# Rearranged operand places, output buffers, weight conversion and store names in a one-core fp32 kernel with two MoE layers

## The chip, the cores and the metric

The kernel runs on one core of one Trainium2 chip. The metric is the device time of one execution in microseconds; lower is better. The engines are named as in the profile: PE (TensorE matmuls; PEld its weight loads), DVE (VectorE), ACT (ScalarE), POOL (GpSimd) and SP (SyncE, whose queue issues nearly all DMAs). Each engine works its own list of instructions in order.

## The reference

Linear attention over 8 batches of 8 heads (576 tokens, head size 64), then two feed-forward layers over 4608 tokens (width 512, inner width 2048), everything in float32. The weights arrive as float64.

```
q_s = exp(q - max(q, -1));  q_s /= sum(q_s, -1) + 1e-9
k_s = exp(k - max(k, seq)); k_s /= sum(k_s, seq) + 1e-9
x = q_s @ (k_s^T @ v)                       # (4608, 512)
h = x @ w_in;  g = h * sigmoid(1.702 * h);  x = g @ w_out          # first layer
h = x @ w2_in; g = max(h, 1) if h >= 1, 0 if h <= -1, else (h + 1)**2 / 4
out = g @ w2_out                                                    # second layer
```

## The kernel before

**Precision and products.** Each fp32 operand is split into a high half (fp32r, a copy on ACT) and a low half (operand minus high half, on DVE), and a product is three matmuls: high·high, high·low, low·high. Most of the matrix products are done in seven block products instead of eight (Strassen's scheme in Winograd's form): the activations are cut into quadrants 11, 12, 21, 22, and the products bear the numbers 1 to 7. Products 7, 6 and 5 need one sum of two quadrants before the split, product 2 one sum after it (for product 4, whose quadrant is 21), products 1, 3 and 4 none. So an operand costs DVE two instructions for products 7, 6, 5, 2 and one for 1, 3, 4.

**The passes, in order of time.** First the attention with the direct product by w_in for four of nine blocks of 512 tokens (`gemm1`, L1038 to L1040). In this pass the converted w_in is also combined into the seven weights (`t_pieces`, through the two buffers `t_raw`, tiles `ts0` and `ts1`; `t3_pieces` makes the weight of product 3, through slot 19). Then *pass 1's pairs* (`gemm_b`, L1367): the other five blocks, in three groups of 2 × 384, 2 × 448, 2 × 448 tokens, each with 4 pieces g of 7 products; the results go through gelu into DRAM (`g0_dram`). Then *pass 2* (`gemm2`, L1519), by w_out of the first layer: 5 groups j of tokens (HALVES: 2 × 512 three times, 2 × 384 twice), each with 7 products in the order 1, 7, 6, 5, 2, 3, 4 and 4 pieces i a product. One *step* is one product and one piece, 12 matmuls; a group has 28 steps. Then two more passes for the second layer (`pass_in`, L605, and `out_pass`, L487), which the diff doesn't touch. The combined weights of the later passes are made during the passes before (`Weights`): a raw load of float64 (L234, L240), a conversion (`conv`, L178 to L191), then sums and splits (`hl`, L282 to L304) whose results go to DRAM (`wp_in`, `wp_out`) and come back as 2 MB loads (`load_weight`, L344). The eight conversions of `in2` lie in pass 2 and use slots 8 to 11 (`W2`).

**SBUF.** Most tiles are numbered slots of [128, 2, 512] fp32. In pass 2 an operand's high and low half take two places of a ring, `RING`, in turn; `at_ring` says which. `GROUPS` are the slots of the quadrants, loaded by `load_g`. Sums of products are kept in the slots that `O_AT` names: c22 (finished at product 5), c11 (product 2), u2, u3. In pass 1's pairs the outputs take their slots from the list `EB`.

**The order.** Nothing is scheduled at run time. All work of the first three passes is put on a list with `add(engine, ns, rank, fn, reads, writes, moves, haste)`, and `Plan.order` writes the engines' queues out by a small simulation: each engine takes, of the pieces that could start first, the one with the lowest rank less haste; a piece waits for the last writer of each name it reads and for writer and readers of each name it writes. Transfers are counted one behind another (`moves`), and 1.9 us are added behind a piece of SP. NEXT is the rank of pass 2's first step, LAST that of pass 1's; `later` puts the conversion behind with a haste of −3. `hand` passes slots from one use to the next. Operands are made LA = 3 ranks ahead of their step.

Of the kernel before, what the change touches and what calls it, by code (L numbers as in the profile page):

```python
# [8 lines left out]
FP32 = mybir.dt.float32  # L9
# [89 lines left out]
def kernel(  # L99
# [15 lines left out]
    P = 128  # L115
# [20 lines left out]

    ident = const.tile([P, P], FP32, name="ident")
    half = const.tile([P, 96], FP32, name="half")[:, :1]
    ctx.enter_context(tc.tile_pool(name="even", bufs=1, side="right")).tile([P, 120], FP32, name="even")


    PROD = (1, 7, 6, 2, 5, 4, 3)
# [240 lines left out]
    def bank(i, name="z"):  # L383
        return rooms["p", i].tile([P, 2, TB], FP32, tag=f"p{i}", name=name)

    O_AT = {"s7": 20, "u2": 21, "c11": 22, "c12": 23, "u3": 20, "c22": 23}
    T_AT = (22, 23)
    C_AT = {p: 4 + 2 * i for i, p in enumerate(PROD)}
    C_AT[PROD[-1]] = 20
# [819 lines left out]
        k, c = AT_W[p]  # L1209
        return ("wh", 4 * c + g, k), ("w", 4 * c + g, k)  # L1210

    t_raw = [sm.tile([P, 512], FP32, tag=f"ts{i}", name=f"ts{i}").rearrange("p (a f) -> p a f", a=2) for i in range(2)]

    def t_pieces(u, g):
        ns = 90 + 1.06 * 512
        rows, k = (2 * g, 2 * g + 2), [u]
        free = tuple(("free", x) for x in ("rq", "fq", "h"))

        def do(engine, fn, reads, writes):
            k[0] += 0.04  # L1220
            add(engine, ns, k[0], fn, reads, writes)

        def part(x):
            return t_raw[x] if isinstance(x, int) else f32(t_at(x[0], *rows)[x[1]])

        def name(x):
            return (("ts", x),) if isinstance(x, int) else w_names(x[0], g)[x[1]:x[1] + 1]

        def dve(o, x, y, op):
            do("DVE", lambda: tt(part(o), part(x), part(y), op), name(x) + name(y), name(o))  # L1230

        def high(p, x):
            do("ACT", lambda: copy(t_at(p, *rows)[0], t_raw[x]), (("ts", x),) + free, w_names(p, g)[:1])

        def low(p, x):
            do("DVE", lambda: tt(t_at(p, *rows)[1], t_raw[x], part((p, 0)), ALU.subtract),
                (("ts", x),) + w_names(p, g)[:1] + free, w_names(p, g)[1:])

        def both(x, y, op):
            dve(0, (x, 0), (y, 0), op)  # L1240
            dve(1, (x, 1), (y, 1), op)
            dve(0, 0, 1, ALU.add)

        both(3, 4, ALU.add)
        high(5, 0)
        dve(1, 0, (1, 0), ALU.subtract)
        dve(1, 1, (1, 1), ALU.subtract)
        high(6, 1)
        low(5, 0)
        low(6, 1)  # L1250
        both(1, 3, ALU.subtract)
        high(7, 0)
        low(7, 0)

    t3 = []

    def t3_pieces(u, g):
        ns, rows, own = 90 + 1.06 * 512, (2 * g, 2 * g + 2), (("t3", g % 2),)

        def at(p, i):  # L1260
            return f32(t_at(p, *rows)[i])

        def mine():
            if not t3:
                t3.append(slot(19))
            return t3[0][:, g % 2].rearrange("p (a f) -> p a f", a=2)

        def step_of(k, x, y, op, names):
            add("DVE", ns, u + k, lambda: tt(mine(), x(), y(), op), names, own)

        step_of(0, lambda: at(2, 0), lambda: at(6, 0), ALU.subtract, w_names(2, g)[:1] + w_names(6, g)[:1])
        step_of(0.1, mine, lambda: at(6, 1), ALU.subtract, own + w_names(6, g)[1:])
        step_of(0.2, mine, lambda: at(2, 1), ALU.add, own + w_names(2, g)[1:])
        to = w_names(3, g)
        add("ACT", ns, u + 0.3, lambda: copy(t_at(3, *rows)[0], mine()), own, to[:1])
        add("DVE", ns, u + 0.4, lambda: tt(t_at(3, *rows)[1], mine(), at(3, 0), ALU.subtract), own + to[:1], to[1:])

    for kind in ("rq", "fq", "h"):
        hand(NM + 0.5, (("free", kind),), tuple((kind, n) for n in range(4)), tuple(("fr", n) for n in range(4)))
    hand(AT[NB - 1][1] + 10.88, sl(19), (('t3', 0), ('t3', 1)))  # L1280
    hand(LAST + 40, (('t3', 0), ('t3', 1)), sl(19))
    for g in range(4):
        t_pieces((20, 29, 38, 47)[g], g)
        t3_pieces(LAST - 2.5 + 4.5 * g, g)


    SRC = {1: "11", 7: "12", 6: "11", 2: "21", 5: "12", 4: "21", 3: "22"}
# [34 lines left out]
    PAIRS = ((384, 0), (448, 768), (448, 1664))  # L1322
    QB = {"11": 20, "12": 21, "22": 22, "21": 23}
    CB = {1: (0, 1), 7: (2, 3), 6: (4, 5), 2: (6, 7), 5: (16, 17), 4: (8, 9), 3: (10, 11)}
    E1, E2 = (24, 25, 26, 18), (19, 20, 21, 22)
    EB = E1 * 4 + (24, 25, 26, 18, 19) * 4
    EB = EB[:32] + (E1 + E2) * 2
    WB = (12, 13, 14, 15)
    x_t, x_ops, zb, tmp_b, e_n = {}, {}, {}, {}, [0]

# [42 lines left out]
    def post_b(s, jj, g, p):  # L1373
# [23 lines left out]
        def finish(make, e, src, src_n, a, t, haste=0):  # L1397
# [9 lines left out]
                for off, m, j, c in parts:  # L1407
                    nc.sync.dma_start(out=g0_dram[j][a * 4 + g][:, :, c], in_=got[0][:, :, off:off + m])

            add("SP", 420 * len(parts), s + 1.3, kept, e, tuple(("g0", x[2]) for x in parts), moves=2.5 * n)  # L1410

        def more(name, a, t):
            e = tmp_b[jj, g, name, "n"]
# [62 lines left out]
    OPENS2 = (1, 7, 5, 4)  # L1476
    GROUPS = tuple(range(12, 16)), tuple(range(4, 8)), tuple(range(4))
    W2 = (8, 9, 10, 11)
    RING = (16, 17, 24, 25, 26, 18, 19)
    LA = 3  # L1480
    steps = [(j, p, i) for j in range(NJ) for p in ORDER for i in range(4)]
    g_t, ops2, zs2, tmp2 = {}, {}, {}, {}
# [7 lines left out]
    def load_g(j, qd, i, rank):  # L1490
# [4 lines left out]
        def fn():  # L1495
# [2 lines left out]
                nc.sync.dma_start(out=t[:, :, off:off + m], in_=g0_dram[jb][h * 4 + i][:, :, c:c + m])  # L1498

        add("SP", 560 * len(parts), rank, fn,  # L1500
            step(int(rank) - 1) + tuple(("g0", jb) for _, _, jb, _ in parts), sl(k), moves=2.5 * n)

    def at_ring(s):
        return tuple(RING[(2 * s + x) % len(RING)] for x in range(2))

    def gemm2(s):
        j, p, i = steps[s]
# [17 lines left out]
    def post2(s, j, p):  # L1525
# [42 lines left out]
            more("c22", "u3")  # L1568
            store("c22", 1, 1)
        elif p == 2:  # L1570
            keep("c11")
            store("c11", 0, 0)
        elif p == 3:
            more("u2", "u2")
            store("u2", 0, 1)
# [12 lines left out]
        load_g(0, "22", i, NEXT - (6.9, 6.8, 5.9, 5.8)[i])  # L1588
        load_g(0, "12", i, NEXT - (4.9, 4.8, 3.9, 3.8)[i])
    w_new2 = Weights("in2", W2)  # L1590
    hand(NEXT + 0.5, sl(*W2), w_new2.names)
    w_new2.everything([NEXT + 3 + 12 * i for i in range(8)], later)
    tail = NEXT + 4 * len(ORDER) * (NJ - 1)
    hand(tail + 3, w_new2.names, sl(*W2))

# [103 lines left out]
```

## Time and profile before

| What | Value |
|---|---|
| median of 3 runs | 1545.35 us (1545.29 to 1548.23) |
| the profiled execution | 1543.8 us, of which the span is 1541.8 us |
| PE busy | 1490.0 us, 97% of the span, 7920 matmuls |
| DVE busy | 1125.3 us, 73% |
| ACT busy | 904.2 us, 59% |
| mean granted clock of PE | 0.995 |
| DMA | 341.16 MB, mean 221 GB/s |

The span runs from the first to the last instruction of the profiled execution; its own time lies 2.0 us above it. A busy time is the union of an engine's instructions, as a share of the span. The line numbers are those of the kernel before; L209 is the helper `tt`, through which all sums and low halves go, and L1190 the helper `copy`.

### The profile page before, as it was taken

Reading aid. Unit: us, or ns where it says so; the run is one execution under the profiler, and the core shown is the slowest. Engines: PE = TensorE matmul, PEld = TensorE weight load, DVE = VectorE, ACT = ScalarE, POOL = GpSimd, SP = SyncE. Lnnn points to the kernel's source line nnn. Section 1 sums busy time; section 2 is a strip of 40 time slices with the busy share of each in tenths; the row PEclk is TensorE's granted clock in tenths of the full one; section 3 lists DMA queues with packets and bytes.
Section 4 is the critical chain, followed back from the end, with each engine's and each line's share of the span. In section 5 each row is a group of like instructions: output and inputs, shape, how many; then the busy total and the mean of one; then the engine's idle time right before and its main releaser. Section 6 shows DMA issues by size and latency. Waiting matters only on the chain.

```text
span 1541.8 us, 21375 instructions
## 1 busy us (share of the span) xinstructions
PE 1490.0 (97%) x7920; PEld 1297.4 (84%) x7920; DVE 1125.3 (73%) x1410; ACT 904.2 (59%) x1140; POOL 6.2 (0%) x27
## 2 busy tenths in 40 slices
PE   5999999999998999999999999999999999999998
PEld 3787777889897778787998788888999888888998
DVE  7999962664617798798776576766774878696885
ACT  5878874565634455554534687777786544343443
POOL 0000000000000000000000000000000000000000
PEclk9999999999999999999999999999999999999999
DMA  9977753878778975767559546464768971534341
GB/s 290 283 222 223 232 185 151 274 235 278 248 282 319 326 260 194 255 189 243 170 193 368 198 180 249 184 225 185 252 221 315 415 250 41 196 101 148 103 124 41
DMA packets 273656, 341.16 MB, mean 221 GB/s; under 512 B 97040, under 2 KB 235792, under 8 KB 270864
## 3 DMA queue, kind: packets, MB, share of 16 engines
q1 hardware_dynamic: 272752, 339.70, 65.1%
q8 instruction: 62, 1.02, 0.3%
q14 instruction: 42, 0.34, 0.1%
q10 hardware_dynamic: 800, 0.10, 0.0%
HBM read 196.08 MB, written 143.65 MB: 220 GB/s over the span
## 4 chain that ended last, share of the span: by engine, by line
PE 77%; DMA 12%; DVE 6%; ACT 2%; issue 2%; SPq 1%; DVEq 0%; ACTq 0%
PE z L605 13%; PE z L487 12%; PE z L1519 10%; PE zx L605 9%; PE zx L487 9%; DVE s L209 5%; PE hps L1038 4%; PE z L1367 4%; PE hps L1040 4%; PE hps L1039 4%; DMA g<-s 3%; PE zx L1367 3%; DMA s<-g 3%; PE zx L1519 3%; DMA wp_in<-s 2%
## 5 line engine op out<-in xcount | busy, mean ns | idle before, releaser
L209 DVE TENSOR_TENSOR s<-s,s 128x1024 fp32r<-128x1024 f32 (+7 forms) x692 | 607.6, 918 | 190.4 <-ACT s L282 40.4
L1519 PE MATMUL z<-s,w 128*128 128x512 f32 (+1 forms) x1440 | 305.3, 370 | 16.4 <-DVE s L209 16.0
L1519 PEld LDWEIGHTS z<-s,w 128*128 128x128 f32 x1440 | 262.3, 189 | 57.3 <-DVE s L209 23.0
L1190 ACT ACTIVATE s<-s 128x1024 fp32r<-128x1024 f32 (+2 forms) x168 | 161.3, 969 | 151.5 <-PE z L1519 89.5
L455 ACT ACTIVATE s<-s 128x1024 fp32r<-128x1024 f32 (+1 forms) x140 | 136.3, 976 | 175.4 <-PE zx L487 62.1
L487 PE MATMUL z<-s,w 128*128 128x512 f32 (+1 forms) x1008 | 210.6, 368 | 0.5 <-DVE s L209 0.5
L605 PE MATMUL z<-s,w 128*128 128x512 f32 (+1 forms) x960 | 207.2, 367 | 2.4 <-ACT s L1190 2.4
L487 PEld LDWEIGHTS z<-s,w 128*128 128x128 f32 x1008 | 183.8, 188 | 25.2 <-DVE s L209 0.9
L605 PEld LDWEIGHTS z<-s,w 128*128 128x128 f32 x960 | 175.0, 188 | 25.2 <-ACT s L1190 2.8
L605 PE MATMUL zx<-s,w 128*128 128x512 f32 (+1 forms) x720 | 157.7, 367 | 0.4 <-issue 0.4
L605 PEld LDWEIGHTS zx<-s,w 128*128 128x128 f32 x720 | 131.3, 188 | 17.6 <-issue 0.8
L487 PE MATMUL zx<-s,w 128*128 128x512 f32 (+1 forms) x648 | 135.1, 367 | 0.0
L487 PEld LDWEIGHTS zx<-s,w 128*128 128x128 f32 x648 | 117.9, 188 | 14.9
L1367 PE MATMUL z<-s,w 128*128 128x448 f32 (+1 forms) x576 | 118.6, 359 | 4.8 <-ACT s L1190 3.7
L1367 PEld LDWEIGHTS z<-s,w 128*128 128x128 f32 x576 | 106.8, 190 | 11.8 <-ACT s L1190 4.4
L1038 PE MATMUL hps<-s,w 128*128 128x512 f32 x256 | 104.7, 409 | 0.2 <-ACT s L1044 0.2
L1040 PE MATMUL hps<-s,w 128*128 128x512 f32 x256 | 100.2, 392 | 0.0
L1039 PE MATMUL hps<-s,w 128*128 128x512 f32 x256 | 100.0, 391 | 0.0
L1367 PE MATMUL zx<-s,w 128*128 128x448 f32 (+1 forms) x432 | 89.2, 357 | 3.2 <-ACT zx L1190 2.2
L282 ACT ACTIVATE s<-s 128x256 fp32r<-128x256 f32 x168 | 64.7, 410 | 38.6 <-DMA wp_in<-s 18.3
L209 DVE TENSOR_TENSOR s<-s,z 128x1024 f32<-128x1024 f32 (+2 forms) x58 | 63.6, 1097 | 32.0 <-PE z L1367 7.4
L1367 PEld LDWEIGHTS zx<-s,w 128*128 128x128 f32 x432 | 78.8, 188 | 9.4 <-ACT zx L1190 3.0
(102 smaller groups left out, 1466.4 us busy)
## 6 DMA issues: line engine op xcount, KB each, us to landing
s<-g SPq DMA_DIRECT2D x96, 512.0 KB, 6.3
g<-s SPq DMA_DIRECT2D x80, 512.0 KB, 2.9
wp_out<-s SPq DMA_DIRECT2D x112, 256.0 KB, 2.9
w<-wp_out SPq DMA_DIRECT2D x14, 2048.0 KB, 12.4
g<-s SPq DMA_DIRECT2D x48, 384.0 KB, 3.7
s<-g SPq DMA_DIRECT2D x48, 384.0 KB, 4.3
s<-in_moe_w_out_dram SPq DMA_DIRECT2D x32, 512.0 KB, 4.7
wp_in<-s SPq DMA_DIRECT2D x56, 256.0 KB, 4.0
```

The lines of the kernel that those rows point to most:

```text
L209: return nc.vector.tensor_tensor(out=o, in0=x, in1=y, op=op)
L282: nc.scalar.activation(out=hi, in_=src, func=ACTF.Copy, scale=-1.0 if neg else 1.0)
L455: first_of[s] = nc.scalar.activation(out=hi, in_=src, func=ACTF.Copy)
L487: nc.tensor.matmul(out=z[:, m, :n], lhsT=a, rhs=b[:, c, :], start=(at is not None and i == 0 and c == 0 and x == 0), stop=(i == 3 and c == ...
L605: nc.tensor.matmul(out=z[:, m, :n], lhsT=a, rhs=b[:, c, :], start=(p in OPENS and c == 0 and x == 0), stop=(c == 1 and x == 2), skip_group ...
L1038: nc.tensor.matmul(out=hps, lhsT=wh, rhs=ah, start=(kk == 0), stop=False)
L1039: nc.tensor.matmul(out=hps, lhsT=wh, rhs=al, start=False, stop=False)
L1040: nc.tensor.matmul(out=hps, lhsT=wl, rhs=ah, start=False, stop=(kk == KD - 1))
L1190: nc.scalar.activation(out=o, in_=x, func=ACTF.Copy)
L1367: nc.tensor.matmul(out=zb[jj, g, a][:, m, :n], lhsT=w[:, f], rhs=y[:, c, :], start=(p in OPENS and c == 0 and x == 0), stop=(c == 1 and x ...
L1519: nc.tensor.matmul(out=zs2[j, a][:, m, :n], lhsT=y, rhs=b[:, c, :], start=(first and c == 0 and x == 0), stop=(i == 3 and c == 1 and x == ...
```

## The change

Seven edits. (1) `t_pieces` and `t3_pieces` work on 256 elements instead of 512, in twice as many pieces; `t_raw` shrinks, and `t3_pieces` uses one new buffer `spare` (the former padding tile `even`, wider) in place of both halves of slot 19. (2) So slot 19 is free for pass 1's first group, and `EB` begins with five output buffers instead of four; in the last list two slots are exchanged. (3) The stores of `g0_dram` get a name for each tile, not for each block, and `load_g` waits for the tile that it reads. (4) `RING` gets slot 22 as eighth place. (5) The sum of product 2 is kept as d11 in slot 23, which c22 also uses. (6) Steps 1 and 2 of pass 2 take slots 8 to 11. (7) The eight conversions of `in2` begin at ranks 17 and 23 of each of the first four groups, instead of every 12 ranks from 3.

```diff
@@ -136,7 +136,7 @@
     half = const.tile([P, 96], FP32, name="half")[:, :1]
-    ctx.enter_context(tc.tile_pool(name="even", bufs=1, side="right")).tile([P, 120], FP32, name="even")
+    spare = ctx.enter_context(tc.tile_pool(name="even", bufs=1, side="right")).tile([P, 376], FP32, name="even")[:, :256]
@@ -383,7 +383,7 @@
-    O_AT = {"s7": 20, "u2": 21, "c11": 22, "c12": 23, "u3": 20, "c22": 23}
+    O_AT = {"s7": 20, "u2": 21, "c11": 22, "c12": 23, "u3": 20, "c22": 23, "d11": 23}
     T_AT = (22, 23)
@@ -1209,11 +1209,11 @@
-    t_raw = [sm.tile([P, 512], FP32, tag=f"ts{i}", name=f"ts{i}").rearrange("p (a f) -> p a f", a=2) for i in range(2)]
...
-    def t_pieces(u, g):
-        ns = 90 + 1.06 * 512
-        rows, k = (2 * g, 2 * g + 2), [u]
+    t_raw = [sm.tile([P, 256], FP32, tag=f"ts{i}", name=f"ts{i}").rearrange("p (a f) -> p a f", a=1) for i in range(2)]
...
+    def t_pieces(u, m):
+        g, ns = m // 2, 90 + 1.06 * 256
+        rows, k = (m, m + 1), [u]
         free = tuple(("free", x) for x in ("rq", "fq", "h"))
@@ -1252,36 +1252,29 @@
-    t3 = []
...
-    def t3_pieces(u, g):
-        ns, rows, own = 90 + 1.06 * 512, (2 * g, 2 * g + 2), (("t3", g % 2),)
+    def t3_pieces(u, m):
+        g, ns, rows, own = m // 2, 90 + 1.06 * 256, (m, m + 1), (("t3",),)
+        x = spare.rearrange("p (a f) -> p a f", a=1)
...
-        def mine():
-            if not t3:
-                t3.append(slot(19))
-            return t3[0][:, g % 2].rearrange("p (a f) -> p a f", a=2)
...
-        def step_of(k, x, y, op, names):
-            add("DVE", ns, u + k, lambda: tt(mine(), x(), y(), op), names, own)
+        def step_of(k, a, b, op, names):
+            add("DVE", ns, u + k, lambda: tt(x, a(), b(), op), names, own)
         step_of(0, lambda: at(2, 0), lambda: at(6, 0), ALU.subtract, w_names(2, g)[:1] + w_names(6, g)[:1])
-        step_of(0.1, mine, lambda: at(6, 1), ALU.subtract, own + w_names(6, g)[1:])
-        step_of(0.2, mine, lambda: at(2, 1), ALU.add, own + w_names(2, g)[1:])
+        step_of(0.1, lambda: x, lambda: at(6, 1), ALU.subtract, own + w_names(6, g)[1:])
+        step_of(0.2, lambda: x, lambda: at(2, 1), ALU.add, own + w_names(2, g)[1:])
         to = w_names(3, g)
-        add("ACT", ns, u + 0.3, lambda: copy(t_at(3, *rows)[0], mine()), own, to[:1])
-        add("DVE", ns, u + 0.4, lambda: tt(t_at(3, *rows)[1], mine(), at(3, 0), ALU.subtract), own + to[:1], to[1:])
+        add("ACT", ns, u + 0.3, lambda: copy(t_at(3, *rows)[0], x), own, to[:1])
+        add("DVE", ns, u + 0.4, lambda: tt(t_at(3, *rows)[1], x, at(3, 0), ALU.subtract), own + to[:1], to[1:])
...
         hand(NM + 0.5, (("free", kind),), tuple((kind, n) for n in range(4)), tuple(("fr", n) for n in range(4)))
-    hand(AT[NB - 1][1] + 10.88, sl(19), (('t3', 0), ('t3', 1)))
-    hand(LAST + 40, (('t3', 0), ('t3', 1)), sl(19))
     for g in range(4):
-        t_pieces((20, 29, 38, 47)[g], g)
-        t3_pieces(LAST - 2.5 + 4.5 * g, g)
+        for m in range(2):
+            t_pieces((20, 29, 38, 47)[g] + m, 2 * g + m)
+            t3_pieces(LAST - 2.5 + 4.5 * g + m, 2 * g + m)
@@ -1322,9 +1315,8 @@
     CB = {1: (0, 1), 7: (2, 3), 6: (4, 5), 2: (6, 7), 5: (16, 17), 4: (8, 9), 3: (10, 11)}
-    E1, E2 = (24, 25, 26, 18), (19, 20, 21, 22)
-    EB = E1 * 4 + (24, 25, 26, 18, 19) * 4
-    EB = EB[:32] + (E1 + E2) * 2
+    E1, E2 = (24, 25, 26, 18), (19, 20, 22, 21)
+    EB = ((24, 25, 26, 18, 19) * 7)[:32] + (E1 + E2) * 2
     WB = (12, 13, 14, 15)
@@ -1407,7 +1399,7 @@
-            add("SP", 420 * len(parts), s + 1.3, kept, e, tuple(("g0", x[2]) for x in parts), moves=2.5 * n)
+            add("SP", 420 * len(parts), s + 1.3, kept, e, tuple(("g0", x[2], a * 4 + g) for x in parts), moves=2.5 * n)
@@ -1476,7 +1468,7 @@
     W2 = (8, 9, 10, 11)
-    RING = (16, 17, 24, 25, 26, 18, 19)
+    RING = (16, 17, 24, 25, 26, 18, 19, 22)
     LA = 3
@@ -1498,10 +1490,12 @@
         add("SP", 560 * len(parts), rank, fn,
-            step(int(rank) - 1) + tuple(("g0", jb) for _, _, jb, _ in parts), sl(k), moves=2.5 * n)
+            step(int(rank) - 1) + tuple(("g0", jb, h * 4 + i) for _, _, jb, _ in parts), sl(k), moves=2.5 * n)
     def at_ring(s):
-        return tuple(RING[(2 * s + x) % len(RING)] for x in range(2))
+        if s in (1, 2):
+            return W2[2 * s - 2], W2[2 * s - 1]
+        return tuple(RING[(2 * max(0, s - 2) + x) % len(RING)] for x in range(2))
@@ -1568,8 +1562,8 @@
         elif p == 2:
-            keep("c11")
-            store("c11", 0, 0)
+            keep("d11")
+            store("d11", 0, 0)
         elif p == 3:
@@ -1588,8 +1582,8 @@
     w_new2 = Weights("in2", W2)
-    hand(NEXT + 0.5, sl(*W2), w_new2.names)
-    w_new2.everything([NEXT + 3 + 12 * i for i in range(8)], later)
+    hand(NEXT + 3.5, sl(*W2), w_new2.names)
+    w_new2.everything([NEXT + 28 * (i // 2) + 17 + i % 2 * 6 for i in range(8)], later)
     tail = NEXT + 4 * len(ORDER) * (NJ - 1)
```

## Rows read from the trace of the kernel before

**Rows 1.** The page, busy us by engine, share of the span, instructions.
```profile
PE 1490.0 (97%) x7920; PEld 1297.4 (84%) x7920; DVE 1125.3 (73%) x1410; ACT 904.2 (59%) x1140; POOL 6.2 (0%) x27
```

**Rows 2.** By stretch (us): busy PE, PEld, DVE, ACT, POOL; clock; DMA share, GB/s.
```profile
31.00:263.94 232.94, 232.78 (x1750) 183.82 (x1749) 191.34 (x271) 178.28 (x203) 3.08 (x10) 1.00 0.74 225
263.94:473.09 209.15, 201.20 (x1022) 187.56 (x1021) 107.11 (x182) 118.87 (x177) 0.00 (x0) 0.99 0.78 264
473.09:843.31 370.22, 352.63 (x1682) 305.79 (x1681) 298.51 (x361) 175.52 (x228) 0.00 (x0) 1.00 0.72 246
```

**Rows 3.** Waits of PE: who waited for whom, us in total, times, longest.
```profile
PE z L1519 <- DVE s L209: 16.0, 16, 1.8
```

**Rows 4.** PE in order of time, pass 2: start, us, shape, count [idle before].
```profile
498.80 5.60 PE L1519 MATMUL z<-s,w 128*128 128x512 f32 x24
504.24 5.60 PE L1519 MATMUL zx<-s,w 128*128 128x512 f32 x24
...
515.12 3.11 PE L1519 MATMUL z<-s,w 128*128 128x512 f32 x13
...
543.15 13.89 PE L1519 MATMUL z<-s,w 128*128 128x512 f32 x60 [0.26 <-DVE s L209]
...
567.29 16.39 PE L1519 MATMUL z<-s,w 128*128 128x512 f32 x71 [1.51 <-DVE s L209]
...
634.70 5.55 PE L1519 MATMUL z<-s,w 128*128 128x512 f32 x16 [1.84 <-DVE s L209]
...
798.23 2.24 PE L1519 MATMUL zx<-s,w 128*128 128x384 f32 x12
800.31 2.24 PE L1519 MATMUL z<-s,w 128*128 128x384 f32 x12
```

**Rows 5.** Stretches of 38 us within pass 2, columns as in rows 2.
```profile
511.00:549.00 38.00, 36.07 (x154) 28.20 (x154) 25.97 (x32) 17.22 (x23) 0.00 (x0) 1.00 1.01 387
...
625.00:663.00 38.00, 36.16 (x152) 29.45 (x151) 30.86 (x38) 17.64 (x23) 0.00 (x0) 0.96 0.62 210
```

**Rows 6.** ACT and SP in order of time, end of pass 1.
```profile
448.97 0.92 ACT L1402 ACTIVATE s<-z 128x896 f32<-128x896 f32 x1 [1.47 <-PE z L1367]
...
458.69 0.80 SPq L1498 DMA_DIRECT2D s<-g  x2
459.58 1.19 SPq L1408 DMA_DIRECT2D g<-s  x2
...
468.19 0.64 SPq L344 DMA_DIRECT2D w<-wp_out  x1
...
475.60 5.65 SPq L234 DMA_DIRECT2D s<-in_moe_w_in_dram  x2
```

**Rows 7.** DVE in order of time, start of pass 2.
```profile
476.54 9.42 DVE L209 TENSOR_TENSOR s<-s,s 128x1024 fp32r<-128x1024 f32 x8 [1.44 <-DMA g<-s]
```

**Rows 8.** ACT and DVE in order of time, group 0 of pass 2.
```profile
516.46 0.42 ACT L282 ACTIVATE s<-s 128x256 fp32r<-128x256 f32 x1 [5.74 <-DMA wp_in<-s]
...
516.91 1.90 DVE L209 TENSOR_TENSOR s<-s,s 128x256 fp32r<-128x256 f32 x3 [5.81 <-ACT s L282]
```

**Rows 9.** DVE in order of time, end of group 1 of pass 2.
```profile
631.16 1.23 DVE L209 TENSOR_TENSOR s<-s,s 128x1024 f32<-128x1024 f32 x1 [5.34 <-DMA s<-g]
```

**Rows 10.** Line 1549 at 529.7, product 5's store in group 0.
```profile
DMA to landing us min/median/max: 12.4/12.4/12.4
```

**Rows 11.** ACT in order of time, first group of pass 1's pairs.
```profile
297.70 0.81 ACT L1190 ACTIVATE s<-zx 128x768 f32<-128x768 f32 x1 [0.35 <-DMA g<-s]
```

**Rows 12.** DVE in order of time: two pairs of instructions, back to back.
```profile
102.40 0.68 DVE L209 TENSOR_TENSOR w<-ts,w 128x512 fp32r<-128x512 f32 x1
103.01 0.68 DVE L888 TENSOR_REDUCE mc<-pa 128x4 f32<-128x512 f32 x1
...
503.20 0.42 DVE L209 TENSOR_TENSOR s<-s,s 128x256 fp32r<-128x256 f32 x1
503.53 0.42 DVE L292 SCALAR_TENSOR_TENSOR s<-s,s 128x256 fp32r<-128x256 f32 x1
```

## Prediction

> **What bounds the kernel now.** I read the page first. PE is busy for 1490.0 of 1541.8 us [rows 1], so only 51.8 us of idle time can be had, and the first question is in which pass it lies. The view by stretches, cut at the passes' first matmuls, says it [rows 2]: in the attention and first product (31 to 264 us) PE idles 232.94 − 232.78 = 0.2 us; in pass 1's pairs 209.15 − 201.20 = 8.0; in pass 2 (the weight w_out1) 370.22 − 352.63 = 17.6. Pass 2 holds the most, and the list of waits says for whom: 16.0 us in 16 waits for DVE, at the line of the helper for sums [rows 3]. These are operands: each step's low half is the last thing made before its twelve matmuls.
>
> Idle time is less than the loss, because after each gap PE's pipe fills again, so I price pass 2 by its steps. Undisturbed, 24 matmuls of 512 columns go from 498.80 to 504.24, 2.72 us a step; of 384 columns from 798.23 to 800.31, 2.08 [rows 4]. Groups 0 to 2 have 84 steps, groups 3 and 4 have 56: 84 × 2.72 + 56 × 2.08 = 345.0 us, against 370.2. **25.2 us are lost in pass 2**, and the change can win no more there. PE's order of time [rows 4], with 0.2267 us a matmul, places them:
> - (a) the start: seven steps before 498.80 take 25.7 us instead of 19.0: 6.7 lost.
> - (b) 515.12 to 543.15, 109 matmuls: 28.0 instead of 24.7: 3.3 lost.
> - (c) all that follows: 15.2 lost by subtraction. [...]
>
> **Why (a) is lost.** SP works its list in order. At 458.69 it issues a quadrant load that had waited for PE, and only behind it, at 459.58, an output store whose gelu ended at 448.97 + 0.92 = 449.89 [rows 6]. The store lies 9.7 us late, and those behind it with it; a 2 MB weight load goes in at 468.19, and at 475.60 two raw loads of the next weight keep SP 5.65 us. Step 1's operand goes to places 24 and 25, which these stores empty: DVE waits 1.44 us for a store until 476.54 [rows 7], and with seven places the steps behind inherit the delay.
>
> **What the change does to (a).** The order list had named a store by its block alone, so each store of a block counted as a successor of the one before; named singly, they can stand right behind their gelu. Steps 1 and 2 go to places 8 to 11, so the late stores don't matter to them. The new wait: 8, 9 come free one step before pass 1's end, 10, 11 at its end, 473.1; a copy and a low half of a 128x1024 operand take about 1.1 + 1.2 us, and step 2 is wanted two steps later, at 478.5, so 3 us are to spare. Raw loads stand no longer there. Step 5 takes 19 and 22, emptied by pass 1's last group, wanted at 486.7. From 0 (the late step 5 keeps the wait) to 6.7; I take 5.5.
>
> **(b): conversion away from the first sixteen steps.** At 516.46 ACT has idled 5.74 us, for a store of converted weights, and DVE 5.81 behind it at 516.91 [rows 8]: both queues stood still, because the store lay in the DMA queue with the weight loads of w_out1. The change's first conversion begins at step 17, so this wait goes; but two conversions now meet the last weight loads and group 1's quadrants. From 0 to 3.3; I take 2.5.
>
> **(c): the eighth place.** With seven places a low half goes into the place of step s−3's high half, with eight both halves go where s−4 stood: one step (2.72 or 2.08 us) earlier. The typical stall is at 631.16: DVE has idled 5.34 us for a quadrant load [rows 9], because a sum of products 7 and 6 for the next group stood in its list before the low halves that PE wanted; those had no place yet. With the place free a step earlier they can stand ahead of the sum, and the gap of 1.84 us at 634.70 [rows 4] is shorter than the 2.72 won. What speaks against all 15.2: the conversions are gathered where quadrants of the next group are loaded, and eight of them still occupy DVE as long as before. Between 0 and 15.2 I take half, 7.5.
>
> **Slot 22 taken, c11 moved to slot 23.** Product 2's sum now waits until product 5's has been stored. In group 0 that store took 12.4 us to land [rows 10]; product 2 ends four steps, 10.9 us, behind product 5. So ACT can wait 1.5 us there, or some 4 with the late issue; ACT's lead hides it, uncovered it costs PE the same. I take 0.5 within the half above.
>
> **Pass 1's parts.** The fifth output buffer spares the first of the three groups of tokens waits for stores. The one of these that I find in front of a gap of PE is 0.35 us, ACT's at 297.70 [rows 11], though 8.0 us are idle in the pass. Stores named singly also move the raw loads of w_out1 in SP's list, either way. From −1 to 2, I take +0.5. The halved sums of weights: 60 more DVE instructions (11 × 4 and 4 × 4) and 16 more on ACT. Back to back, a 128x512 takes 0.61 us from start to start (102.40, 103.01), a 128x256 takes 0.33 (503.20, 503.53) [rows 12]: 0.06 more a pair, 3 to 4 us in all; by whole durations (2 × 0.42 − 0.68 = 0.16) 9.6. DVE's 232.94 − 191.34 = 41.6 free us before pass 1 [rows 2] and its half-free pass 1 hide either; uncovered, at most 9.6 on PE. I take 0. The one spare buffer makes t3's eight chains serial, four sums of 0.42 us and a copy each, spread over seventeen steps of the pass: hidden.
>
> [...]
>
> **Sum.** 5.5 + 2.5 + 7.5 + 0.5 = 16.0 us. The profiled execution took 1543.8 us (1541.8 of span and 2.0 around it); 1527.8 would be left. The runs' median, 1545.35, lies 1.55 higher, so 1529.4: I say 1530, 1.0% faster. Its own range: gain of 9 to 24, 1521 to 1536.
>
> **Rivals.**
> - *Smaller gain, the DMA queue at the groups' ends.* Twelve steps (32.6 us) now carry a next group's twelve quadrants, three output stores, and two conversions (four raw loads of 512 KB, fourteen stores of 256 KB): about 13.6 MB, 418 GB/s. The fullest stretch moved 387 at a share of 1.01; 625 to 663 moved 210 at 0.62, which is 339 at full [rows 5]. The backlog is between 2.6 and 7.6 us. An idle DVE would wait that much longer for the quadrants, and the eighth place gives 2.72. With 3 to 4 us (c) wins little: (a) and (b) alone, 8 us, 1537 and up to 1542.
> - *Slower, the same backlog at its upper end.* Beyond 2.7 us each of the four group ends pays; 8 us of gain from (a) and (b) are used up at 2.7 + 2 = 4.7. With 7.6 the four cost 19.6 and the time is 1557; with 6, 1551. For it: quadrant loads already keep DVE waiting 5.34 us. Against: the conversion's share of DVE delays the sums too, so that they wait less; and the order list, which books every transfer, will spread them.
> - *The halved sums come late.* DVE's 41.6 free us may lie behind the place where the sums stand; if the attention falls 3 to 9.6 us behind, 1533 to 1540. Against: PE idled 0.2 us in that whole pass [rows 2].
> - *The change doesn't do what it says.* Waits only change hands: steps 1 and 2 wait for pass 1's end, product 2 for slot 23, and the total stays: 1544 to 1547.
>
> [...]
>
> **Chances.** Forecast 0.52, smaller gain 0.17, late sums 0.06, no change 0.10, slower 0.15. A change of 0.2%, 3.1 us, is what a measurement tells from none: faster 0.75, same 0.10, slower 0.15. The range 1521 to 1547 leaves out most of the slower case and a little below.
>
> **What would show it.** Right: pass 2 within 350 to 358 us, no wait over 0.5 us in its first seven steps, no 5 us of idle DVE behind converted weights in group 0, no fall of the clock in pass 2. Wrong for (c): DVE's waits for quadrants at steps 26 to 30 of a group are longer than 5.34 us and PE's gaps there over 1.84, with a DMA share near 1. Wrong for the halving: gaps before 264 us. Wrong altogether: PE's idle in pass 2 still 17 us, with other owners.

## The result, and the profile after

The kernel after takes **1528.9 us** (median of four runs, 1526.43 to 1529.44) against 1546.07 before in the same series: ratio 0.9884, 95% interval 0.9867 to 0.9901. That is 17.2 us or 1.1% faster; forecast were 1530 us and 16.0 us. The profiled execution of after is the slowest of the four, 1529.44 us with a span of 1527.4.

The page of after, busy time, share of the span and instructions of each engine:

```profile
PE 1487.4 (97%) x7920; PEld 1296.8 (85%) x7920; DVE 1132.3 (74%) x1470; ACT 903.4 (59%) x1154; POOL 6.2 (0%) x27
```

Beside [rows 1] DVE has 60 instructions and 7 us more. The span fell by 14.4 us and PE's busy time by only 2.6, so the rest was idle time of PE. Where it was shows in the stretches, cut at the passes' first matmuls (attention, pass 1's pairs, pass 2, then `pass_in`; columns as in [rows 2]):

```profile
31.00:265.86 234.86, 233.46 (x1752) 184.01 (x1751) 200.31 (x327) 179.55 (x217) 3.08 (x10) 1.00 0.75 224
265.86:472.84 206.98, 202.15 (x1021) 187.80 (x1020) 107.31 (x189) 119.99 (x180) 0.00 (x0) 0.99 0.80 276
472.84:830.00 357.16, 348.88 (x1683) 305.64 (x1682) 300.15 (x363) 175.87 (x229) 0.00 (x0) 1.00 0.73 250
830.00:1176.40 346.40, 345.59 (x1681) 305.23 (x1680) 232.03 (x300) 259.74 (x321) 0.00 (x0) 1.00 0.61 225
```

Against [rows 2] the attention is 1.9 us longer, pass 1 2.2 shorter and pass 2 13.1 shorter, 13.3 in all; the 1.1 left of 14.4 lies in the two passes behind, which the diff doesn't touch. Pass 2 was priced at 345.0 us undisturbed, so 12.2 of its 25.2 us of loss remain. The waits of PE in pass 2 (who waited for whom, us in total, times, longest):

```profile
PE z L1513 <- DVE s L209: 5.8, 10, 1.3
...
PE z L1513 <- ACT s L1190: 2.5, 2, 1.6
```

The 16.0 us for DVE in [rows 3] are 5.8, and a wait for ACT has come. PE in order of time says where (start, us, shape, count, [idle before]):

```profile
273.82 3.78 PE L1359 MATMUL zx<-s,w 128*128 128x384 f32 x12 [2.94 <-ACT zx L1190]
...
472.84 19.25 PE L1513 MATMUL z<-s,w 128*128 128x512 f32 x84
491.93 2.88 PE L1513 MATMUL zx<-s,w 128*128 128x512 f32 x12
...
510.97 46.41 PE L1513 MATMUL z<-s,w 128*128 128x512 f32 x204
557.77 2.56 PE L1513 MATMUL z<-s,w 128*128 128x512 f32 x10 [0.39 <-DVE s L209]
...
788.84 8.48 PE L1513 MATMUL z<-s,w 128*128 128x384 f32 x48
798.89 0.44 PE L1513 MATMUL z<-s,w 128*128 128x384 f32 x1 [1.57 <-ACT s L1190]
```

The first 84 matmuls, seven steps, take 19.1 us to the next start: the 6.7 us lost at the start of pass 2 in [rows 4] are gone, and so is the loss behind 515. Around group 0's end, where [rows 4] has gaps of 0.26 and 1.51, there is one of 0.39. Most of what remains lies in group 4, whose 28 steps of 2.08 us take 9.8 us too long, 7.7 of them behind 788.84. The 38 us stretches (columns as in [rows 5]) say the same:

```profile
511.00:549.00 38.00, 38.00 (x169) 31.44 (x168) 30.33 (x35) 19.78 (x24) 0.00 (x0) 1.00 1.01 388
...
625.00:663.00 38.00, 37.42 (x165) 30.70 (x164) 33.80 (x40) 18.92 (x24) 0.00 (x0) 1.00 0.46 161
...
777.00:815.00 38.00, 33.39 (x185) 31.60 (x184) 27.97 (x35) 15.21 (x21) 0.00 (x0) 1.00 0.92 328
```

From 511 to 549 PE never idles at the DMA share, 1.01, at which it idled 1.9 us in [rows 5]; from 777 to 815 it idles 4.6 us.

### The profile page after: what moved, and what is told of

Same layout as the page of the kernel before. It is cut to its first block, busy times and chain, and to the rows that moved or that the text cites. A ratio compares the mean times of both kernels' runs of the same rounds, so it can differ in the third digit from the quotient of the medians.

```text
span 1527.4 us, 21403 instructions
## 1 busy us (share of the span) xinstructions
PE 1487.4 (97%) x7920; PEld 1296.8 (85%) x7920; DVE 1132.3 (74%) x1470; ACT 903.4 (59%) x1154; POOL 6.2 (0%) x27
## 4 chain that ended last, share of the span: by engine, by line
PE 79%; DMA 10%; DVE 5%; SPq 2%; issue 2%; ACT 2%; DVEq 0%; ACTq 0%
PE z L605 12%; PE z L487 12%; PE z L1513 12%; PE zx L605 9%; PE zx L487 9%; DVE s L209 4%; PE hps L1038 4%; PE z L1359 4%; PE hps L1040 4%; PE hps L1039 4%; PE zx L1513 3%; PE zx L1359 3%; DMA s<-in_moe_w_out_dram 2%; DMA wp_in<-s 1%; DMA g<-s 1%
## 5 line engine op out<-in xcount | busy, mean ns | idle before, releaser
L209 DVE TENSOR_TENSOR s<-s,s 128x256 fp32r<-128x256 f32 (+6 forms) x692 | 608.0, 918 | 170.2 <-ACT s L1190 42.4
L655 ACT ACTIVATE s<-s 128x1024 f32<-128x1024 f32 (+1 forms) x80 | 77.3, 969 | 1.1
```

What stands on the lines that cost most here:

```text
L209: return nc.vector.tensor_tensor(out=o, in0=x, in1=y, op=op)
L655: nc.scalar.activation(out=got["t"], in_=got["t"], func=ACTF.Square)
```

## The experiments

All kernels in one table, in us. The losses of pass 2 are its steps' starts against 2.72 us a step of 512 columns and 2.08 of 384, as in the prediction; "start" is the first seven steps, "g0" the rest of group 0. Pass 1 and pass 2 and the losses are of the profiled execution alone, medians and ratios of the timed runs (ratio to the kernel before on the same chip, with its 95% interval). A group's loss can hold more than idle time. In the traces of before and after PE's granted clock is either 1.00 or 0.50 of full speed, and in before it is at the lower level for 3.4 us from 635.7. Behind a gap the matmuls also take a little longer: in before twelve of 512 columns take 3.01 and 3.06 us (477.82, 518.87), without a gap 2.88 (509.68).

| kernel | median | ratio | pass 1 | pass 2 | start | g0 | g1 | g2 | g3 | g4 |
|---|---|---|---|---|---|---|---|---|---|---|
| before | 1546.07 | 1 | 209.1 | 370.2 | 6.7 | 4.0 | 5.6 | 1.5 | 5.0 | 2.5 |
| after | 1528.90 | 0.9884 [0.9867, 0.9901] | 207.0 | 357.2 | 0 | 0 | 0.7 | 0.2 | 1.3 | 9.8 |
| e1_conv_spread | 1520.59 | 0.9837 [0.9822, 0.9851] | 204.6 | 350.0 | 0 | 0 | 0 | 1.2 | 1.7 | 1.9 |
| e2_seven_places | 1539.92 | 0.9961 [0.9947, 0.9975] | 207.2 | 371.4 | 1.5 | 1.9 | 5.9 | 1.5 | 8.6 | 6.9 |
| e3_start_in_ring | 1528.33 | 0.9883 [0.9868, 0.9898] | 205.7 | 356.8 | 0 | 0 | 0.5 | 0.2 | 1.6 | 9.3 |
| e4_store_names | 1534.47 | 0.9925 [0.9910, 0.9940] | 205.9 | 365.2 | 8.2 | 0 | 0.6 | −0.6 | 1.3 | 10.6 |
| e5_pieces_512 | 1535.14 | 0.9923 [0.9903, 0.9943] | 212.3 | 358.2 | 0 | 0.4 | 0.7 | 0.1 | 1.2 | 10.7 |
| e6_conv_alone | 1549.91 | 1.0020 [1.0007, 1.0033] | 211.1 | 373.2 | 6.4 | 1.1 | 3.7 | 1.9 | 8.6 | 6.3 |
| e7_eighth_alone | 1531.52 | 0.9899 [0.9882, 0.9915] | 210.4 | 357.0 | 8.1 | 0.1 | 0 | 0.8 | 1.2 | 1.6 |
| e8_last_earlier | 1527.42 | 0.9878 [0.9860, 0.9897] | 207.3 | 357.3 | 0 | 0 | 0.5 | 0.2 | 8.6 | 2.8 |
| e9_four_buffers | 1529.57 | 0.9884 [0.9868, 0.9901] | 212.2 | 351.3 | 0 | 0 | 0.9 | 0.7 | 2.4 | 2.2 |
| e10_none_in_group3 | 1523.61 | 0.9849 [0.9833, 0.9864] | 206.3 | 350.6 | 0 | 0 | 0.2 | 0.8 | 2.7 | 1.6 |
| e11_loads_later | 1527.41 | 0.9877 [0.9862, 0.9892] | 206.4 | 352.1 | 0 | 0 | 0 | −0.1 | 1.8 | 5.2 |
| e12_t3_later | 1521.41 | 0.9835 [0.9811, 0.9860] | 208.4 | 354.5 | 0 | 0 | 0.3 | 5.1 | 1.8 | 2.2 |

Profiles of kernels that differ in pass 2 alone differ in pass 1 too: it took 204.6 to 207.3 us in after, e1, e2, e8, e10 and e11. The rows e1 and e12 say more. Every engine has the same list of operations, tiles and shapes in both, yet pass 1 lies 3.8 us apart and pass 2 4.5, most of it in group 2 (the profiled execution of e12, 1527.81 us, is the slowest of its four). So differences below 4 us of pass 1 are not read, and a smaller one of pass 2 than that counts only where the rows show which gap came or went.

**e1_conv_spread: after, with the conversions spread again.** The first starts at rank 5, the others every 12 ranks.

```diff
-    w_new2.everything([NEXT + 28 * (i // 2) + 17 + i % 2 * 6 for i in range(8)], later)
+    w_new2.everything([NEXT + 5 + 12 * i for i in range(8)], later)
```

> The changed kernel with its conversions spread over pass 2 again, every 12 ranks, from rank 5. My theory (three causes: the start, conversions away from the w_out1 loads, the eighth place): the 3.3 us of (b) come back and part of (c), while groups 3 and 4, which now lose 10 us, win some 3 back: 1531 to 1537, pass 2 at 359 to 366 us. Rival A (the placement of the conversions makes the whole gain of pass 2, the eighth place none): 1540 to 1544, pass 2 at 368 or more. Rival B (the eighth place makes it all): 1526 to 1530.

1520.59 us, below all three ranges. That is 8.3 below after (7.3 by the ratios), and the intervals of the two ratios don't touch. Pass 2 by stretches:

```profile
468.90:818.90 350.00, 347.15 (x1683) 305.77 (x1682) 300.65 (x364) 177.34 (x229) 0.00 (x0) 1.00 0.75 255
```

Group 4 loses 1.9 us instead of 9.8, and group 0 still nothing. Gathering the conversions wins nothing in this kernel; it costs 7.2 us of pass 2. No kernel measured here has a lower median.

**e2_seven_places: after, with seven places in the ring.**

```diff
-    RING = (16, 17, 24, 25, 26, 18, 19, 22)
+    RING = (16, 17, 24, 25, 26, 18, 19)
```

> The changed kernel with seven places in the ring (slot 22 unused). My theory: half of the loss behind the start comes back, 6 to 10 us: 1535 to 1539, with gaps of over 1 us at the groups' ends behind sums that wait for quadrants. Rival A: 1528 to 1530, no new gaps. Rival B: 1540 or more.

11.0 us slower than after, pass 2 as long as before the change. PE's wait for DVE is back:

```profile
PE z L1513 <- DVE s L209: 12.3, 9, 2.8
```

The gaps stand around the groups' ends again: 1.65 us at 545.63, 2.83 at 626.02, 1.80 at 705.91 and 2.35 at 718.20, 1.79 at 771.78. Four times in pass 2 PE's granted clock is at its lower level for 3.4 us (from 626.1, 718.2, 772.8 and 813.8); by estimate, half of these 13.6 us, 6.8, are lost on top of the gaps. The matmuls there (107 from 626.02, 59 from 718.20, 96 from 771.78 and 96 from 813.26) take 1.7 to 1.9 us longer than as many do undisturbed, and the mean granted clock of pass 2 is 0.98. After has no such time in pass 2, with a mean of 1.00.

**e3_start_in_ring: after, steps 1 and 2 in the ring.**

```diff
-        if s in (1, 2):
-            return W2[2 * s - 2], W2[2 * s - 1]
-        return tuple(RING[(2 * max(0, s - 2) + x) % len(RING)] for x in range(2))
+        return tuple(RING[(2 * s + x) % len(RING)] for x in range(2))
```

> The changed kernel with steps 1 and 2 in the ring (places 24, 25 and 26, 18) instead of slots 8 to 11. My theory: with the stores named singly these places are empty in time, so little comes back: 1529 to 1532. Rival (it is the slots 8 to 11 that mend the start): the 6.7 us of the first seven steps come back, 1534 to 1536.

1528.33 us, as after, and PE's first 72 matmuls of pass 2 run on without a gap:

```profile
471.18 16.51 PE L1511 MATMUL z<-s,w 128*128 128x512 f32 x72
```

**e4_store_names: after, with stores named by their block.**

```diff
-            add("SP", 420 * len(parts), s + 1.3, kept, e, tuple(("g0", x[2], a * 4 + g) for x in parts), moves=2.5 * n)
+            add("SP", 420 * len(parts), s + 1.3, kept, e, tuple(("g0", x[2]) for x in parts), moves=2.5 * n)
...
-            step(int(rank) - 1) + tuple(("g0", jb, h * 4 + i) for _, _, jb, _ in parts), sl(k), moves=2.5 * n)
+            step(int(rank) - 1) + tuple(("g0", jb) for _, _, jb, _ in parts), sl(k), moves=2.5 * n)
```

> The changed kernel with stores and loads named by block again. My theory: steps 1 and 2 no longer need the stores, but steps 3 to 5 do: 1530 to 1534, with the loss in the first seven steps at 1 to 5 us. Rival (the names alone make the start): 6 to 7 us come back, 1535 to 1536. Second rival (the slots alone make it): 1528 to 1530.

5.6 us slower than after, and the whole loss of the start is back (8.2), though steps 1 and 2 lie in slots 8 to 11. PE in order of time:

```profile
481.54 3.04 PE L1513 MATMUL z<-s,w 128*128 128x512 f32 x12 [2.50 <-DVE s L209]
...
490.75 4.37 PE L1513 MATMUL zx<-s,w 128*128 128x512 f32 x11 [1.37 <-DVE s L209]
```

SP's list shows the difference. In after, all but three of the last stores go in ahead of the 2 MB weight load at 470.82:

```profile
441.33 15.82 SPq L1400 DMA_DIRECT2D g<-s  x9
458.15 8.23 SPq L1490 DMA_DIRECT2D s<-g  x8
466.55 4.22 SPq L1400 DMA_DIRECT2D g<-s  x3
470.82 0.61 SPq L344 DMA_DIRECT2D w<-wp_out  x1
473.52 2.27 SPq L1400 DMA_DIRECT2D g<-s  x3
```

and in e4 nine of them follow the load at 465.38, four of these a second one:

```profile
465.38 0.32 SPq L344 DMA_DIRECT2D w<-wp_out  x1
466.67 8.96 SPq L1400 DMA_DIRECT2D g<-s  x5
475.68 1.74 SPq L344 DMA_DIRECT2D w<-wp_out  x1
477.52 4.00 SPq L1400 DMA_DIRECT2D g<-s  x4
```

So the single names win the start, and the slots of steps 1 and 2 add nothing that can be measured. The raw loads, which the prediction named too, are not the cause: without them there and with the old names 6.4 us are lost (e6), and e1, where two raw loads stand in SP's list at 477.29, loses nothing.

**e5_pieces_512: after, without the halved sums of weights and without the fifth buffer** (edits 1 and 2 undone; the exchange of two slots stays).

```diff
-    t_raw = [sm.tile([P, 256], FP32, tag=f"ts{i}", name=f"ts{i}").rearrange("p (a f) -> p a f", a=1) for i in range(2)]
+    t_raw = [sm.tile([P, 512], FP32, tag=f"ts{i}", name=f"ts{i}").rearrange("p (a f) -> p a f", a=2) for i in range(2)]
...
-    EB = ((24, 25, 26, 18, 19) * 7)[:32] + (E1 + E2) * 2
+    EB = E1 * 4 + (24, 25, 26, 18, 19) * 4
+    EB = EB[:32] + (E1 + E2) * 2
```

> The changed kernel with the weight sums in pieces of 512 again, the sums of product 3 in slot 19, and four output buffers in the first group of pass 1. My theory from the two traces: the first pass ends 1.9 us earlier (60 DVE instructions less), pass 1 loses about as much: 1527 to 1531. Rival (the buffer pays and the halving is hidden, as I had predicted): 1529 to 1532. Second rival (the halving costs, the buffer gives nothing): 1525 to 1527.

6.2 us slower than after, above all three ranges; pass 1 takes 5.3 us longer, and the losses of pass 2 stay within 0.9 us of after's. So the two edits together win some 5 us in pass 1.

**e6_conv_alone: before, with only the conversions moved** (edit 7 alone, the line of e1's diff).

> The kernel before with the conversions moved, and nothing else. My theory: (b) is won and part of (c) is not, the start wins a little since no raw loads stand there, groups 3 and 4 lose 4: 1538 to 1543. Rival A (placement is all): 1532 to 1535. Rival B (the eighth place is all): 1545 to 1550.

Ratio 1.0020 [1.0007, 1.0033], slower than before. The rest of group 0 loses 1.1 us instead of 4.0: PE runs 157 matmuls from 517.61 without a gap, where before it stopped four times, from 518.87 to 543.15. So the collision that edit 7 moves out of group 0 was real; but groups 3 and 4 lose 14.9 instead of 7.5.

**e7_eighth_alone: before, with only the eighth place** and what it needs, the sum of product 2 in slot 23 (edits 4 and 5, and the exchange of two slots in pass 1's list).

```diff
-    O_AT = {"s7": 20, "u2": 21, "c11": 22, "c12": 23, "u3": 20, "c22": 23}
+    O_AT = {"s7": 20, "u2": 21, "c11": 22, "c12": 23, "u3": 20, "c22": 23, "d11": 23}
...
-    E1, E2 = (24, 25, 26, 18), (19, 20, 21, 22)
+    E1, E2 = (24, 25, 26, 18), (19, 20, 22, 21)
...
-    RING = (16, 17, 24, 25, 26, 18, 19)
+    RING = (16, 17, 24, 25, 26, 18, 19, 22)
...
-            keep("c11")
-            store("c11", 0, 0)
+            keep("d11")
+            store("d11", 0, 0)
```

> The kernel before with the eighth place, d11 in slot 23 and the two slots of the output list exchanged, and nothing else. My theory: half of (c) is won, the start and (b) stay: 1536 to 1541. Rival A: 1544 to 1548. Rival B: 1531 to 1534.

1531.52 us: alone it wins 14.0 of after's 17.2 us (15.6 of 17.9 by the ratios). The start of pass 2 is as bad as before, and behind it PE hardly stops, the stretch from 515 to 543 with the conversions in their old place included:

```profile
480.06 12.52 PE L1519 MATMUL z<-s,w 128*128 128x512 f32 x47 [2.21 <-DVE s L209]
...
521.06 39.15 PE L1519 MATMUL z<-s,w 128*128 128x512 f32 x172
```

Behind the start 18.6 us were lost before and 3.7 are now. DVE's waits in pass 2 show by what way. Before, it waited for PE to use up an operand, and then for quadrants:

```profile
DVE s L209 <- PE z L1519: 20.4, 20, 2.2
DVE s L209 <- DMA s<-g: 12.8, 5, 5.3
```

In e7 the first wait is all but gone and the second less than half:

```profile
DVE s L209 <- DMA s<-g: 5.0, 4, 2.9
DVE s L209 <- PE z L1519: 1.6, 3, 1.0
```

With the eighth place DVE is ahead of PE, as the prediction's (c) said. Some of the waits for PE can be for its results instead of for a place; the list doesn't tell the two apart.

**e8_last_earlier: after, with conversions at ranks 17, 23, 45, 51, 73, 79, 88 and 101,** so that the last one ends six ranks sooner.

```diff
-    w_new2.everything([NEXT + 28 * (i // 2) + 17 + i % 2 * 6 for i in range(8)], later)
+    w_new2.everything([NEXT + x for x in (17, 23, 45, 51, 73, 79, 88, 101)], later)
```

> The changed kernel with the seventh and eighth conversion at ranks 88 and 101 instead of 101 and 107. In the trace after the change groups 3 and 4 lose 11 us of pass 2's 12, and behind the late last conversion two 2 MB loads of the next pass go in within 2.3 us, ahead of the quadrants 21. If the late last conversion is the cause, 4 to 8 us of it go: 1521 to 1525. Rival (groups 3 and 4 of 384 columns are too short for DVE wherever the conversions lie, or the 2 MB loads meet the quadrants anyhow): 1527 to 1530.

1527.42 us, no better than after. The loss has moved from group 4 (9.8 to 2.8) to group 3 (1.3 to 8.6), where the longest gap is

```profile
764.09 11.07 PE L1513 MATMUL z<-s,w 128*128 128x384 f32 x46 [2.86 <-DVE s L209]
```

At this gap the granted clock is at its lower level for 6.8 us from 763.5 (the mean of pass 2 is 0.99), so by estimate 3.4 of the 8.6 us are the clock. So "the last one ends too late" was not all of it.

**e9_four_buffers: e1, with four output buffers for the first group of pass 1** (the two lines of `EB` in e5's diff; the halved sums stay).

> The kernel with the conversions every 12 ranks (1520.6 us in an earlier run), but with four output buffers in the first group of pass 1's pairs; the weight sums stay in pieces of 256. Pass 1 took 205 to 207 us in the runs with both edits, 212 without both. If the fifth buffer makes the difference: pass 1 at 209 to 212 us, 1524 to 1527. If the small pieces make it (smaller instructions between the low halves, slot 19 not needed): pass 1 stays at 205 to 207, 1519 to 1522.

1529.57 us, 9.0 above e1 (7.3 by the ratios) and above both ranges. 7.6 of it lie in pass 1, 3.8 to 7.6 against all kernels with five buffers. The chain there, in order of time on ACT, DVE and PE:

```profile
346.36 0.92 ACT L1190 ACTIVATE s<-zx 128x896 f32<-128x896 f32 x1 [2.60 <-DMA g<-s]
```
```profile
354.37 1.09 DVE L209 TENSOR_TENSOR s<-s,s 128x896 f32<-128x896 f32 x1 [5.97 <-DMA s<-xs]
```
```profile
356.51 6.69 PE L1360 MATMUL zx<-s,w 128*128 128x448 f32 x24 [3.79 <-DVE s L209]
```

ACT waits 2.60 us for a store to empty a buffer, DVE 5.97 us for the next quadrant, and PE 3.79. In e1 no such gap stands in pass 1; e5, with four buffers too, has PE's at 355.80 with 2.77 us. That the halved sums stay and pass 1 is as long as in e5 (212.2 and 212.3) says that the buffer, not the size of the pieces, makes the difference. That the quadrant is late because of the buffer is read from the order in time; no run took it apart.

**e10_none_in_group3: after, with all eight conversions in groups 0 to 2.**

```diff
-    w_new2.everything([NEXT + 28 * (i // 2) + 17 + i % 2 * 6 for i in range(8)], later)
+    w_new2.everything([NEXT + x for x in (5, 17, 23, 40, 45, 51, 73, 79)], later)
```

> The changed kernel with all eight conversions in groups 0 to 2 (ranks 5, 17, 23, 40, 45, 51, 73, 79), closer together still. Theory 1 (what costs is a conversion in the groups of 384 columns, and the late last one, not the gathering): groups 3 and 4 lose 4 us at most instead of 11, 1519 to 1523. Theory 2 (gathering costs wherever it is): groups 0 to 2 lose 4 or more instead of 0.9, 1523 to 1530.

1523.61 us, 5.3 below after; pass 2 takes 350.6 us, as in e1. Groups 0 to 2 carry all eight and lose 1.0 us together, and groups 3 and 4, without any, 4.3 instead of 11.1. So what costs is two conversions in group 3, and not that they are gathered. A step of that group has 2.08 us instead of 2.72; that this is why is argued, not shown.

**e11_loads_later: after, with the weight loads of the next pass behind products 7 and 6 six ranks later.**

```diff
-            load_w2(w_in2, "in2", PROD[ORDER.index(p)], ORDER.index(p), r + 1)
+            load_w2(w_in2, "in2", PROD[ORDER.index(p)], ORDER.index(p), r + 1 + 6 * (p in (7, 6)))
```

> The changed kernel with the second and third 2 MB load of w2_in six ranks later in the order list, behind the quadrants 21 of the last group; the conversions stay gathered. Theory 1a (group 4 stalls because the late conversion pushes 2 MB loads ahead of the quadrants): group 4 loses 2 to 5 us instead of 9.8, 1521 to 1525. Theory 1b (DVE is full in these groups): 1527 to 1530, group 4 at 8 or more. If the later loads are missed by the next pass, 1530 or more, with gaps in the first 30 us of that pass.

To see why, first SP in after:

```profile
778.80 4.53 SPq L301 DMA_DIRECT2D wp_in<-s  x4
788.93 0.34 SPq L344 DMA_DIRECT2D w<-wp_in  x1
789.37 1.71 SPq L1490 DMA_DIRECT2D s<-g  x2
791.18 0.56 SPq L344 DMA_DIRECT2D w<-wp_in  x1
791.80 9.60 SPq L1490 DMA_DIRECT2D s<-g  x6
```

The last conversion's stores go out until 783.3, and two 2 MB loads stand behind them, in between and ahead of the eight loads of the last quadrant, 21. ACT in after:

```profile
798.00 0.84 ACT L1190 ACTIVATE s<-s 128x768 fp32r<-128x768 f32 x1 [6.51 <-DMA s<-g]
```

It idles 6.51 us for a quadrant, and PE stops at 798.89. In e11 group 4 loses 5.2 instead of 9.8, and PE runs through there; pass 2 is 5.1 us shorter. But the time is 1527.41, as after: `pass_in` takes 352.0 us instead of 346.4, and PE stops in it once for long.

```profile
787.11 31.53 PE L1513 MATMUL z<-s,w 128*128 128x384 f32 x181
...
842.97 0.79 PE L605 MATMUL zx<-s,w 128*128 128x512 f32 x1 [4.60 <-ACT s L1190]
```

So the place of the two loads makes 4.6 of the 9.8 us. The row at 842.97 doesn't say that the moved loads are late: the copy that PE waits for stands behind four activations in ACT's list, the first of which had waited 2.42 us for a sum of DVE. That the later loads cost `pass_in` its 5.6 us is argued, not shown. The rest of group 4's loss wasn't traced.

**e12_t3_later: e1, with the weight of product 3 made three ranks later,** to find the cause of the gap of 2.94 us that every kernel with halved sums shows in the first steps of pass 1 (in after at 273.82; before and e5 have 1.18 us there, and then 1.05).

```diff
-            t3_pieces(LAST - 2.5 + 4.5 * g + m, 2 * g + m)
+            t3_pieces(LAST + 0.5 + 4.5 * g + m, 2 * g + m)
```

> The kernel with the conversions every 12 ranks from 5, and the sums of product 3's weight three ranks later, so that none stands ahead of pass 1's first products. After the change the first gap of pass 1 is 2.94 us (two of 1.18 and 1.05 before), for a copy of ACT that comes behind a conversion which waits 1.34 us for DVE. If the smaller, serial pieces are the cause: that gap is 1.2 us or less, and the time 1517 to 1520. Rival (the order of the conversions there is the cause, the pieces only stand beside it): gap still near 2.9, 1519 to 1522. If the later sums are missed: a gap at product 3 within the first 20 us of pass 1.

The gap is 2.94 us again, and the median 1521.41 as e1's. The pieces stayed where they were in the engines' lists, which are e1's throughout: the order takes what could start first when DVE is free, and the later rank changed nothing. So this run tests neither theory. ACT in e12, with a copy of such a piece (tile `even`) still ahead of the copy that PE waits for:

```profile
268.64 0.40 ACT L1190 ACTIVATE w<-even 128x256 fp32r<-128x256 f32 x1
271.00 0.42 ACT L282 ACTIVATE s<-s 128x256 fp32r<-128x256 f32 x1 [1.34 <-DVE s L209]
271.32 0.79 ACT L1190 ACTIVATE zx<-z 128x768 f32<-128x768 f32 x1
```

The copy into `zx` begins behind a conversion's copy that waited 1.34 us for DVE. This speaks for DVE's list being fuller there, but no run has shown it; the cause of this gap stays open.

## Why the prediction was right

The total was right, 16.0 us against 17.2 by the medians and 14.4 by the profiles, and faster by over 0.2% came true. Three of its terms were off by several us, one of them in sign, and they cancel; that the sum came so near is luck, not the account of where the time lies.

**(a), the start of pass 2: right in size, half right in cause.** Forecast 5.5, won 6.7 of 6.7. The late store was the cause, and naming stores singly cures it: without the names 8.2 us are lost (e4). That steps 1 and 2 had to leave the ring as well was wrong: without that edit nothing is lost (e3). The eighth place has a part in it: with seven 1.5 us come back (e2). The late step 5, for which 1.2 us were taken off, was not seen.

**(b), the conversions: the wrong sign.** Forecast +2.5. The wait was there, and moving the conversions takes 2.9 us of it away when nothing else is done (e6 against before, rest of group 0). But beside the eighth place it is gone anyway (e7: 0.1 lost in the rest of group 0). And the price was missed: after against e1 the move costs 8.3 us, and alone it makes the kernel slower. The step that failed is the sentence that two conversions now meet the last weight loads and group 1's quadrants: I looked for the collision in groups 0 and 1, and priced it at nothing below zero. It came in groups 3 and 4, where a step is 2.08 us and where the 2 MB loads of the next pass share SP's queue with the quadrants. Of the two, only the loads were tried by a run (e11: 4.6 of the 9.8 us of group 4). That these loads come behind the conversions' stores was not in my account.

**(c), the eighth place: the mechanism right, the size half of the true one.** I took 7.5 of 15.2. Alone it takes the loss behind the start from 18.6 to 3.7 us, (b) included (e7); taken out of after it costs 11.0 (e2). One step of lead against gaps of at most 1.84 us was worth nearly all, as the argument for it said; the halving for the conversions' share of DVE was wrong. The rest of "What would show it" agrees: pass 2 takes 357.2 us, PE's clock doesn't fall in it, its first seven steps have no wait over 0.5 us, and DVE waits in pass 2 at most 0.7 us for a conversion's copy (5.8 before) and 1.3 for a quadrant (5.3). The wait for slot 23 (d11), priced at 0.5, shows nowhere: e7 has it too and loses 0.1 in the rest of group 0. With seven places gaps of PE come back around the groups' ends, in before with waits for DVE of up to 1.8 us [rows 3], in e2 of 1.65 to 2.83; with eight the gaps of after at the ends of groups 0 to 2 are 0.39, 0.58 and 0.34 us (557.77, 632.08, 707.66), and of the 5.1 us that PE waits for DVE in pass 2 of e7 3.3 lie at its start.

So (b) and (c) together were 10.0 by forecast. Before and after measure 18.6 − 12.0 = 6.6: some 15 from the place, some 8 lost to the move.

**The fifth buffer: mis-sized.** Forecast +0.5, from −1 to 2. Pass 1 is only 2.2 us shorter than before; but beside the other edits the buffer is worth some 4 to 7.6 us of the pass and 7 to 9 of the time (e9 against e1). With four buffers the kernels of the change have 212.2 and 212.3 in pass 1, those with the old names and pieces 209.1 to 211.1. I had found one wait of 0.35 us for a store [rows 11] and stopped there. ACT's list of waits in pass 1 before would have shown seven:

```profile
ACT s L1190 <- DMA g<-s: 9.4, 7, 2.0
```

In after it is one of 0.7 us, in e9 six of 7.2 us together. By the order in time of e9, a wait of ACT for a store reaches PE by way of later operands.

**The halved pieces: put at nothing, and not quite nothing.** The sums take 0.418 us for 256 elements, as taken from [rows 12], and DVE is busy 9.0 us more before pass 1 (200.31 against 191.34), near the 9.6 by whole durations. In the attention this is hidden, as forecast: pass 1 begins at 263.8 to 265.9 us in the kernels that have them and at 263.9 to 264.7 in the four that don't. At the start of pass 1 it isn't. The first five steps there take 16.0 us in before, e5, e6 and e7, 17.4 in e9, which has the halved pieces without the fifth buffer, and 17.4 to 19.2 in all ten kernels that have them. So 1.4 us go by the halved pieces, and up to 3.2 where the granted clock falls behind the gap. So of the two terms that the prediction put at nothing, the halved sums and the serial chains of t3, one at least was not hidden; which of them makes the gap of 2.94 us is open (e12).

**The rivals.** The DMA queue at the groups' ends did not cost what the smaller gain and the slower rival wanted: 625 to 663 ran at a share of 0.46, and DVE's longest wait at group 1's end is 1.75 us, for raw weights and not for a quadrant:

```profile
627.51 0.43 DVE L184 TENSOR_SCALAR s<-s 128x512 uint32<-128x512 uint32 x1 [1.75 <-DMA s<-in_moe_w_in_dram]
```

But their mechanism, quadrants late in a full queue, did happen at one place, in group 4, behind weight loads and not behind conversions, with 6.51 us of ACT's wait; by e11 it makes 4.6 of the 9.8 us lost there. It was priced for four ends; it came at one.

## What to carry to other kernels

Count the places for operands in whole operands: seven places for operands of two each, half an operand short, cost 11 to 14 of 1545 us here, and the eighth place for the engine that feeds PE was worth more than any order of the work that was tried. When work is moved away from one collision, look at the stretch where it now ends, here the groups with shorter steps, where big loads wait for its last store; undo each part of a gain, because a part that costs 8 us can hide in a change that wins 17. What an order list takes for a dependence (a name too wide) delays transfers as a real one does: with stores named by block nine stores go in behind a weight load instead of three, and 8.2 us are lost at the start of pass 2 (e4).

## What the runs showed of the hardware

The DMA queues were full without any stall of PE: in after, 511 to 549 moved 388 GB/s at a share of 1.01 while PE was busy for 38.00 of 38.00 us.

The gap of 2.94 us in the first steps of pass 1 is the same in ten kernels, but not what follows. In after twelve matmuls behind it take 3.78 us, and the granted clock is at its lower level (0.50 of full speed) for 3.4 us from 273.5; in e1 they take 4.21, with the lower level for 6.8 us from 271.5. In e2, e9 and e11 twelve matmuls behind the same gap take 2.36 to 2.38 us, and the clock stays at the upper level (1.00):

```profile
272.55 2.38 PE L1360 MATMUL zx<-s,w 128*128 128x384 f32 x12 [2.94 <-ACT zx L1190]
```

That row is e9's, PE in order of time. So a gap of one length cost time at the lower clock in seven executions, where the twelve take 3.72 to 4.21 us, and none in three. Gaps of 1.79 to 2.83 us in e2 were followed by such a time too, one of 1.80 at 705.91 was not.
